# A recurrence with a MoE behind it: b's own load buffer, earlier load requests, and pair rows evicted into the tile that they were made from

## The chip, the cores and the metric

One core of one Trainium2 chip runs the whole kernel in one launch. The metric is device microseconds of that launch. The engines go by short names: PE (TensorE, matrix multiply; PEld is its weight load), DVE (VectorE), ACT (ScalarE), POOL (GpSimd) and SP (SyncE, which here only issues DMA transfers). Each engine takes its own list of instructions in order.

## The reference

Per batch and head (4 x 8 = 32 of them) a state of 40 x 40 is carried over 768 time steps; the outputs go through a feed-forward layer with a piecewise activation.

```
for t in range(S):
    y[:, :, t] = einsum('bhd,bhde->bhe', r_t, state)
    Sa = einsum('bhde,bhe->bhd', state, a_t)
    state = state * w_t[:, :, None, :] - einsum('bhd,bhe->bhde', Sa, b_t) + einsum('bhd,bhe->bhde', v_t, k_t)
x = y as (batch * time, 320)
h = x @ w_in                      # 320 -> 2048
g = h if h >= 1, 0 if h <= -1, else (h + 1)^2 / 4
out = g @ w_out                   # 2048 -> 320
```

## The kernel before, in words

The recurrence is done in chunks of 32 steps (24 chunks), so that inside a chunk it is matrix products, with a unit triangular system to invert. Four chunks (128 steps) make a segment; there are six segments, 0 to 5. Segments 0 and 1 are prepared by code of their own ahead of the main loop (`early_load`, `early_products`, `early_turn`, `early_ab`, `early_store`); segments 2 to 5 go through three background generators that run beside the main loop.

**Rows** (`prelude`, lines 217 to 262). For a segment, decayed and rescaled versions of k, w, a and b are worked out in four parts of eight steps each. Tiles of 128 x 8 x 40 are loaded by `load` (line 225, on SP) into buffers of one copy each: `ld_w`, `ld_a`, `ld_k`. b has no buffer; it is loaded into `ld_a`, after a's last use. Per part: two copies of r and v in DRAM (`copy_rv`, line 123, SP); the running product P of w on DVE (lines 239 and 240 carry over from the part before and need the new a and w, line 243 goes on); `at` on POOL (245); the load of b (247); reciprocal and its running product `rec` on DVE (249, 252); `kt` on POOL (255); `bt` on POOL (257); the store of all four from one tile, `arena`, to a DRAM scratch (258, on POOL's DMA queue); then the loads of the next part's w, a and k (261). Lines 239 and 240 of the next part write `arena` again and so also wait for that store.

**Pairs** (`ab_set`, lines 276 to 309). For a chunk, a and b rows are read back into `tiab` (`load_rows`, line 274, four transfers on SP), turned by four DVE transposes of 128 x 256 into `ea` (287, one buffer, tag "ea"), multiplied pair by pair on PE (298, 32 matmuls into one bank of PSUM), copied by ACT into a tile `ab` (303, one buffer) and stored by four transfers on SP to the DRAM scratch `abd` (306). As soon as the transposes are emitted, the next chunk's `tiab` load is queued.

**Inverse** (`invert`, lines 311 to 336). A segment's triangular systems are loaded (316), solved by 62 operations on POOL (326 and 332; DVE for segment 0) and stored (335).

**The main loop** (lines 847 to 892) runs, per chunk and half of the heads, `chain` (six stages of PE matmuls at lines 468, 479, 497, 526 and 536, with evictions by DVE at 486, 504 and 509 and by ACT at 473, 490, 530 and 538), `scores` (PE 438, DVE 447), `turn` (DVE transposes 423, 426 and 428) and the loads for the chunks to come (`load_ti`, `load_cg`: lines 274, 398, 401, 409). Every 64 steps `relayout` queues nine transfers X<-Y on SP (552, 558, 562) that make the MoE's input. The MoE's matmuls (607 into `ph`, 581 and 585 into `po`, with evictions at ACT 613 and 614, DVE 620, ACT 594 and POOL 595) are fed into PE's list between the chain's stages, a fixed number of columns a step.

The order is written by hand: the pool's own scheduling is off, and the order in which the Python code emits instructions is the order on each engine. The background generators `yield` a cost after each piece (`ROWS_W`, `AB_W`, `INV_W`, and literals), and `background` draws, in each third of a step, from whichever generator is furthest behind its share of a window of steps (`WINDOWS`). Rows of a segment run beside the pairs of the segment before for segments 3 to 5; the last pairs, of segment 5, run alone. The costs only place the emission; they are not times.

The weights of the MoE are loaded and split into two parts by another generator, `weights`, which lends its staging room from tiles that are idle at that time (`reclaim` takes them back).

Of the kernel before, what the change touches and what calls it, by code (L numbers as in the profile page):

```python
# [9 lines left out]
F32 = mybir.dt.float32  # L10
# [18 lines left out]
    ab=[(0, 0), (38, 53), (68, 89), (108, 129), (147, 169)],  # L29
# [20 lines left out]
def rwkv_moe_kernel(ctx: ExitStack, tc: tile.TileContext, r, k, v, w, a, b, w_in, w_out, ident_d, mask_d, out):  # L50
# [8 lines left out]
    const = ctx.enter_context(tc.tile_pool(name="const", bufs=1))  # L59
# [7 lines left out]

    ident = const.tile([128, D], F32, name="ident")
    mask = const.tile([128, 32], F32, name="mask")
    half_c = const.tile([128, 1], F32, name="half_c")  # L70
    nc.gpsimd.memset(half_c, 0.5)
    zero_c = const.tile([128, 1], F32, name="zero_c")
    nc.gpsimd.memset(zero_c, 0.0)

    x_tile = lambda i, t: const.tile([128, 6, 256], t, name=f"X{i}", tag=f"X{i}")
# [16 lines left out]
    work = ctx.enter_context(tc.tile_pool(name="work", bufs=1))  # L92
# [10 lines left out]
    def pad_rows(x, n):  # L103
        for q in (1, 3):
            zero(x[32 * q : 32 * q + 32, :, n : n + 32], 32 * q)
# [14 lines left out]
    def copy_rv(s, part, c):  # L120

        x, o = ((r, O_R), (v, O_V))[part]
        nc.sync.dma_start(
            scr4[s][c, :, :, o : o + D], x.rearrange("b h (n t) e -> (b h) n t e", t=L)[:, 4 * s + c]
        )

    def pad_scr(s):
        nc.sync.dma_start(scr[s][NH * 128 : NH * 128 + 1, 0:D], r[0, 0, 0:1, :])
# [88 lines left out]
    def prelude(s):  # L217

        reclaim(8)
        R = arena.rearrange("p (t x) -> p t x", x=160)  # L220
        kt, P, at, bt = (R[:, :, 40 * i : 40 * i + 40] for i in range(4))

        def load(n, part, tag):
            t = work.tile([128, 8, D], F32, tag=f"ld_{tag}", name=f"ld_{n}")
            nc.sync.dma_start(t, srcs[n][:, 4 * s : 4 * s + 4, 8 * part : 8 * part + 8, :])
            return t

        wl, al, kl = load("w", 0, "w"), load("a", 0, "a"), load("k", 0, "k")
        pad_scr(s)
        yield 10  # L230
        for part in range(4):
            ts_ = slice(8 * part, 8 * part + 8)
            for i in range(2):
                copy_rv(s, i, part)
            if part == 0:
                for x, y in ((P, wl), (at, al)):
                    nc.vector.tensor_scalar(out=x[:, 0], in0=y[:, 0], scalar1=-1.0, scalar2=None, op0=ALU.mult)
            else:
                nc.vector.tensor_mul(at[:, 0], al[:, 0], P[:, 7])
                nc.vector.tensor_mul(P[:, 0], wl[:, 0], P[:, 7])  # L240
            for t in range(1, 8):
                yield 0.4
                nc.vector.tensor_mul(P[:, t], P[:, t - 1], wl[:, t])
            yield ROWS_W[0]
            nc.gpsimd.tensor_mul(at[:, 1:], al[:, 1:], P[:, :7])
            yield ROWS_W[1]
            bl = load("b", part, "a")
            rec = work.tile([128, 8, D], F32, tag="ld_rec", name="rec")
            nc.vector.reciprocal(rec[:, 7], P[:, 7])
            yield 0.6  # L250
            for t in range(7, 0, -1):
                nc.vector.tensor_mul(rec[:, t - 1], rec[:, t], wl[:, t])
                yield 0.4
            yield ROWS_W[2]
            nc.gpsimd.tensor_mul(kt, kl, rec)
            yield ROWS_W[3]
            nc.gpsimd.tensor_mul(bt, bl, rec)
            nc.gpsimd.dma_start(scr[s][0 : NH * 128, 80:240].rearrange("(p t) x -> p t x", t=L)[:, ts_, :], R)
            yield ROWS_W[4]
            if part < 3:  # L260
                wl, al, kl = load("w", part + 1, "w"), load("a", part + 1, "a"), load("k", part + 1, "k")
            yield ROWS_W[5]

    def load_rows(dst, c, off, n, h0=0, nh=NH):

        sc = scr[c // 4]
        for f in range(2):
            for q in range(2):
                row = (h0 + f) * 128 + 32 * (c % 4)
                m = n - 32 * q  # L270
                src = bass.AP(
                    sc.tensor, sc.offset + row * RW + off + 32 * q, [[RW, 32], [256 * RW, nh // 2], [1, m]]
                )
                nc.sync.dma_start(dst[64 * f + 32 * q : 64 * f + 32 * q + 32, :, 0:m], src)  # L274

    def ab_set(s):

        if 9 in lending:
            reclaim(9)
            pad_rows(tiab, 48)  # L280
        load_rows(tiab, 4 * s, O_A, 80)
        yield AB_W[4]
        for c in range(4 * s, 4 * s + 4):
            ea = work.tile([128, 16, 2, 32], F32, tag="ea", name="ea")
            tv = tiab.rearrange("p h (j x) -> p h j x", x=40)[:, :, :, 0:32]
            for i in range(4):
                nc.vector.transpose(ea[:, 4 * i : 4 * i + 4], tv[:, 4 * i : 4 * i + 4])
                yield AB_W[0]
            if c < 4 * s + 3:
                load_rows(tiab, c + 1, O_A, 80)  # L290
            yield AB_W[1]
            ps = psum()
            for p in range(16):
                for f in range(2):
                    rows = slice(64 * f, 64 * f + D)
                    q = 2 * f + p % 2
                    sl = p // 2
                    nc.tensor.matmul(
                        ps[32 * q : 32 * q + 32, 32 * sl : 32 * sl + 32],
                        lhsT=ea[rows, p, 0, :], rhs=ea[rows, p, 1, :], start=True, stop=True,  # L300
                    )
            ab = work.tile([128, 8, 32], F32, tag="ab", name="ab")
            nc.scalar.copy(ab, ps[:, 0:256].rearrange("p (s x) -> p s x", x=32))
            yield AB_W[2]
            for q in range(4):
                nc.sync.dma_start(
                    abd[c // 4][q // 2, c % 4, q % 2 :: 2].rearrange("h t i -> t h i"), ab[32 * q : 32 * q + 32]
                )
            yield AB_W[3]
# [28 lines left out]
    def staged(key, needs, work_of):  # L338
# [12 lines left out]
    done, size, spent = dict(rows=1, ab=1), dict(rows=10 + 4 * (6.2 + sum(ROWS_W)), ab=AB_W[4] + 4 * (4 * AB_W[0] + sum(AB_W[1:4])), inv=INV_W + 67), {}  # L351
    back = {k: staged(*a) for k, a in dict(
        rows=("rows", None, prelude), ab=("ab", "rows", ab_set), inv=("inv", "ab", invert)).items()}

    def drain(key, s):
# [365 lines left out]
    def reclaim(kind):  # L721

        lending.discard(kind)
        while any(x[0] == kind for x in sts.values()):
            next(wgen)
# [10 lines left out]
    load = lambda q: loader[0](q)  # L736
# [189 lines left out]
```

## Time and profile before

| what | us |
|---|---|
| three timed runs | 978.39 median, 973.5 to 979.82 |
| the profiled execution, its own time | 976.18 |
| its span in the trace | 974.4 |
| PE busy in the span | 775.0 (80%) |
| DVE, ACT, POOL busy | 590.4, 478.6, 443.8 |
| mean granted TensorE clock | 0.85 of full |

Lines of the profile read as follows. In a timeline a row has start and length in us, engine, source line, operation, what it writes and reads (`out<-in`), the shapes, how many instructions are merged (x4), and in brackets how long the engine was idle before the first of them and what ended that idle time. A list of waits has who waited, what for, the total in us, how often, and the longest. "SPq" is SP issuing a transfer; the time beside it is that of issuing, not of the transfer.

### The profile page before, as it was taken

Reading aid. Unit: us, or ns where it says so; the run is one execution under the profiler, and the core shown is the slowest. Engines: PE = TensorE matmul, PEld = TensorE weight load, DVE = VectorE, ACT = ScalarE, POOL = GpSimd, SP = SyncE. Lnnn points to the kernel's source line nnn. Section 1 sums busy time; section 2 is a strip of 40 time slices with the busy share of each in tenths; the row PEclk is TensorE's granted clock in tenths of the full one; section 3 lists DMA queues with packets and bytes.
Section 4 is the critical chain, followed back from the end, with each engine's and each line's share of the span. In section 5 each row is a group of like instructions: output and inputs, shape, how many; then the busy total and the mean of one; then the engine's idle time right before and its main releaser. Section 6 shows DMA issues by size and latency. Waiting matters only on the chain.

```text
span 974.4 us, 35827 instructions
## 1 busy us (share of the span) xinstructions
PE 775.0 (80%) x14976; PEld 692.1 (71%) x14976; DVE 590.4 (61%) x1562; ACT 478.6 (49%) x1230; POOL 443.8 (46%) x673
## 2 busy tenths in 40 slices
PE   4523543447886988799879798989999999999995
PEld 3312532336776887688879687978898899999995
DVE  7782876574756583775654774776665556655321
ACT  5822444212543544454445454546565566656663
POOL 5200223686331599332588232697235962222332
PEclk9755555575997789797999796999999999999998
DMA  8799995565677755896735886856855545552010
GB/s 274 148 193 245 202 207 151 141 139 134 146 156 152 163 138 115 178 186 130 179 100 117 182 160 133 173 135 131 146 115 121 110 101 111 105 90 56 16 36 14
DMA packets 276866, 134.64 MB, mean 138 GB/s; under 512 B 194984, under 2 KB 266856, under 8 KB 276704
## 3 DMA queue, kind: packets, MB, share of 16 engines
q1 hardware_dynamic: 273504, 121.20, 57.9%
q0 software_dynamic: 3200, 11.14, 3.8%
q8 instruction: 118, 1.93, 0.9%
q14 instruction: 44, 0.36, 0.1%
HBM read 96.83 MB, written 33.82 MB: 134 GB/s over the span
## 4 chain that ended last, share of the span: by engine, by line
PE 34%; DMA 16%; POOL 16%; DVE 12%; issue 8%; SPq 8%; ACT 4%; POOLq 0%; ACTq 0%; DVEq 0%
PE ph L607 11%; PE po L581 6%; POOL lw L326 5%; POOL lw L332 4%; DMA ti<-scr 4%; PE po L585 3%; PE p L497 3%; POOL gl L595 3%; SPq L274 3%; PE p L468 3%; PE p L526 2%; DMA ld_a<-in_a_dram 2%; PE p L438 2%; PE p L479 2%; PE p L536 1%
## 5 line engine op out<-in xcount | busy, mean ns | idle before, releaser
L607 PE MATMUL ph<-X,w 120*128 120x256 f32 x1536 | 260.9, 307 | 51.6 <-DVE qt L620 44.3
L595 POOL TENSOR_TENSOR gl<-qt,gh 128x256 fp32r<-128x256 f32 x192 | 140.9, 734 | 280.0 <-ACT gh L594 264.6
L607 PEld LDWEIGHTS ph<-X,w 120*128 120x128 f32 x1536 | 219.8, 203 | 68.1 <-DVE qt L620 51.3
L620 DVE SCALAR_TENSOR_TENSOR qt<-qt,ph 128x256 f32<-128x256 f32 x192 | 79.9, 416 | 150.3 <-ACT qt L614 148.3
L581 PE MATMUL po<-wide,gh 128*128 128x320 f32 x768 | 163.7, 329 | 0.3 <-ACT gh L594 0.3
L594 ACT CAST gh<-qt 128x256 fp32r<-128x256 f32 x192 | 78.0, 406 | 167.6 <-DVE qt L620 166.7
L581 PEld LDWEIGHTS po<-wide,gh 128*128 128x128 f32 x768 | 124.6, 202 | 3.7 <-ACT gh L594 0.5
L613 ACT ACTIVATE qt<-ph,half_c 128x256 f32<-128x256 f32 x192 | 91.1, 474 | 53.4 <-POOL gl L595 39.7
L585 PE MATMUL po<-wide,gl 128*128 128x320 f32 x384 | 99.6, 338 | 17.6 <-POOL gl L595 17.6
L497 PE MATMUL p<-cg 128*64 128x72 f32 (+1 forms) x1536 | 74.8, 262 | 44.2 <-DVE cg L486 39.7
L497 PEld LDWEIGHTS p<-cg 128*64 128x64 f32 x1536 | 66.8, 166 | 54.3 <-ACT cg L490 45.0
L326 POOL TENSOR_TENSOR lw<-lw 128x31 f32<-128x31 f32 (+15 forms) x155 | 94.4, 609 | 18.0 <-DMA lw<-abd 9.3
L490 ACT ACTIVATE cg<-p 32x160 f32<-32x160 f32 x192 | 56.8, 296 | 87.9 <-DVE cg L486 61.0
L447 DVE TENSOR_TENSOR cg<-p,mask 32x256 f32<-32x256 f32 x192 | 80.6, 420 | 25.8 <-PE p L438 23.2
L332 POOL TENSOR_TENSOR lw<-lw 128x31 f32<-128x31 f32 (+15 forms) x155 | 84.1, 543 | 8.8
L504 DVE SCALAR_TENSOR_TENSOR cg<-p,pr 40x160 f32<-40x160 f32 x184 | 59.1, 321 | 41.1 <-PE p L497 39.2
L614 ACT ACTIVATE qt<-qt 128x256 f32<-128x256 f32 x192 | 80.2, 418 | 6.1
L585 PEld LDWEIGHTS po<-wide,gl 128*128 128x128 f32 x384 | 65.6, 197 | 23.9 <-POOL gl L595 21.5
L468 PE MATMUL p<-cg 128*64 128x72 f32 x1536 | 66.4, 243 | 16.7 <-DMA cg<-ttd 15.0
L486 DVE SCALAR_TENSOR_TENSOR cg<-p,mask 32x128 f32<-32x128 f32 x192 | 55.2, 288 | 36.2 <-PE p L479 30.7
L468 PEld LDWEIGHTS p<-cg 128*64 128x64 f32 x1536 | 58.7, 149 | 23.6 <-issue 19.0
L526 PE MATMUL p<-ident,cg 40*64 40x40 f32 x1472 | 57.1, 238 | 1.9 <-issue 1.9
(104 smaller groups left out, 1027.9 us busy)
## 6 DMA issues: line engine op xcount, KB each, us to landing
ti<-scr SPq DMA_DIRECT2D x96, 200.0 KB
ti<-scr SPq DMA_DIRECT2D x96, 168.0 KB
scr<-arena POOLq DMA_DIRECT2D x16, 640.0 KB, 5.4
cg<-scr SPq DMA_DIRECT2D x96, 80.0 KB
X<-Y SPq DMA_DIRECT2D x36, 160.0 KB
scr<-wide SPq DMA_DIRECT2D x8, 640.0 KB
tiab<-scr SPq DMA_DIRECT2D x32, 160.0 KB
scr<-in_r_dram SPq DMA_DIRECT2D x24, 160.0 KB
```

Of the source, the lines that this page charges most:

```text
L326: eng.tensor_mul(t3, W3[:, 0:n, j : j + 1].broadcast_to([128, n, m]), L3[:, j + 1 :, j].unsqueeze(1).broadcast_to([128, n, m]),)
L332: eng.tensor_sub(W3[:, 0:n, j + 1 :], W3[:, 0:n, j + 1 :], t3)
L447: nc.vector.tensor_tensor(out=cg[q, f::2, C_X : C_X + 64][:, 4 * i : 4 * i + 4].rearrange("p h (j x) -> p h j x", x=32), in0=ps[quarter(f, ...
L468: nc.tensor.matmul(psv[h // 8][64 * (1 - f) : 64 * (1 - f) + 64, h // 2 % 4, 0:72], lhsT=cg[:, h, C_T : C_T + 64], rhs=cg[:, h, C_R : C_R ...
L497: nc.tensor.matmul(psv[h // 8][64 * f : 64 * f + 64, h // 2 % 4, 0:n3], lhsT=cgw[:, h * CW + C_G : h * CW + C_G + 64], rhs=cg[:, h, C_R : ...
L581: nc.tensor.matmul(pos[i], lhsT=gh[:, ts_], rhs=w2[f // 8][:, j, f % 8, :], start=f == 0 and j == 0, stop=False)
L585: nc.tensor.matmul(pos[i], lhsT=gl[:, ts_], rhs=w2[f // 8][:, 0, f % 8, :], start=False, stop=f == NF - 1)
L595: nc.gpsimd.tensor_sub(gl, gt, gh.bitcast(F32))
L607: nc.tensor.matmul(ph, lhsT=w1[:, wi, fs], rhs=Xs[g][:, xi, :], start=i == 0, stop=i == 7)
L613: nc.scalar.activation(gt, ph, AF.Relu, bias=half_c, scale=0.5)
L614: nc.scalar.activation(gt, gt, AF.Square)
L620: nc.vector.scalar_tensor_tensor(out=gt, in0=gt, scalar=1.0, in1=ph, op0=ALU.min, op1=ALU.max)
```

## The change

The load buffers become four: b's loads go into `ld_b`. A part's b is no longer asked for in the middle of the part but with the loads of the part before (or, for part 0, at the start). The next part's loads are asked for one by one: a after the last `rec` product is emitted, w after `kt`, k and b after `bt` and the store. The planner's costs and the number of yields stay as they were, so everything else is emitted in the same order.

In the pairs, the tile `ab` goes; the PSUM bank is copied into the first half of `ea`, over rows that the matmuls have read, and the four stores read from there. The two constants 0.5 and 0 share one tile of two columns.

```
-    half_c = const.tile([128, 1], F32, name="half_c")
+    consts = const.tile([128, 2], F32, name="consts")
+    half_c, zero_c = consts[:, 0:1], consts[:, 1:2]
...
-        wl, al, kl = load("w", 0, "w"), load("a", 0, "a"), load("k", 0, "k")
+        wl, al, kl, bl = (load(n, 0, n) for n in "wakb")
...
             nc.gpsimd.tensor_mul(at[:, 1:], al[:, 1:], P[:, :7])
             yield ROWS_W[1]
-            bl = load("b", part, "a")
             rec = work.tile([128, 8, D], F32, tag="ld_rec", name="rec")
...
+            more = part < 3
+            if more:
+                al = load("a", part + 1, "a")
             yield ROWS_W[2]
             nc.gpsimd.tensor_mul(kt, kl, rec)
+            if more:
+                wl = load("w", part + 1, "w")
             yield ROWS_W[3]
             nc.gpsimd.tensor_mul(bt, bl, rec)
             nc.gpsimd.dma_start(scr[s][0 : NH * 128, 80:240].rearrange("(p t) x -> p t x", t=L)[:, ts_, :], R)
             yield ROWS_W[4]
-            if part < 3:
-                wl, al, kl = load("w", part + 1, "w"), load("a", part + 1, "a"), load("k", part + 1, "k")
+            if more:
+                kl, bl = load("k", part + 1, "k"), load("b", part + 1, "b")
             yield ROWS_W[5]
...
-            ab = work.tile([128, 8, 32], F32, tag="ab", name="ab")
+            ab = ea.rearrange("p a j x -> p (a j) x")[:, 0:8]
             nc.scalar.copy(ab, ps[:, 0:256].rearrange("p (s x) -> p s x", x=32))
```

More of the change, by code (lines that the diff above doesn't have):

```diff
@@ L69, in rwkv_moe_kernel @@
     mask = const.tile([128, 32], F32, name="mask")
-    half_c = const.tile([128, 1], F32, name="half_c")
+    consts = const.tile([128, 2], F32, name="consts")
+    half_c, zero_c = consts[:, 0:1], consts[:, 1:2]
     nc.gpsimd.memset(half_c, 0.5)
-    zero_c = const.tile([128, 1], F32, name="zero_c")
     nc.gpsimd.memset(zero_c, 0.0)
```

## The prediction

> **What bounds the kernel now.** I read the page first, then a table of stretches, then the list of waits, then the timeline around each wait that the change removes or adds.
>
> ```profile
> span 974.4 us, 35827 instructions
> ...
> PEclk9755555575997789797999796999999999999998
> ...
> scr<-arena POOLq DMA_DIRECT2D x16, 640.0 KB, 5.4
> ```
> ```profile
> 708.00:728.00 20.00, 20.00 (x438) 18.15 (x440) 12.11 (x34) 13.39 (x36) 5.62 (x8) 1.00 0.57 118
> 728.00:912.00 184.00, 181.48 (x3672) 164.54 (x3668) 105.92 (x282) 110.36 (x292) 83.02 (x130) 0.99 0.44 93
> ```
>
> From 728 us on, PE is busy 181.48 us of 184 at a granted clock of 0.99, and nothing that the change touches runs any more after the last rows and pairs are done. (Columns: the stretch and its length, busy time of PE, PEld, DVE, ACT and POOL, granted clock, DMA share, GB/s.) Before that PE has holes, and the clock row of the page dips with them. Every engine here runs a fixed list in order, so a hole in PE moves the end by its length, and a wait on another engine costs only what reaches PE. That is the rule by which I price everything below.
>
> ```profile
> DVE arena L239 <- DMA ld_a<-in_a_dram: 24.9, 5, 12.1
> ...
> POOL arena L257 <- DMA ld_b<-in_b_dram: 18.4, 7, 6.9
> DVE ea L287 <- DMA tiab<-scr: 18.4, 6, 6.0
> ...
> ACT ab L303 <- DMA abd<-ab: 5.6, 2, 4.1
> ```
>
> (Columns: us in total, times, the longest.) The first two lines are what the change goes for: DVE waits 24.9 us in five places for the next part's a, POOL 18.4 us in seven for b. The fourth goes too: the eviction waited twice for the old tile's stores. The third says that DVE already sits at the pair transposes until a load lands: the very place where the change puts one wait more.
>
> **What the change removes.** The 16 parts of the rows (segments 2 to 5, four each) issue the same 64 loads and as many vector instructions; only their places differ. With b in its own buffer, a load of a is queued after the reciprocals, w after the k product, k and b after the b product, so no part waits for its own b, and a and w stand several planner units earlier in SP's queue. Issuing costs the same; the two constants in one tile cost nothing, for nothing in the loops writes them. At the start of a segment's rows one load more (b) is queued behind w, a and k, and is not the one that is waited for first.
>
> I go through the waits that end.
>
> ```profile
> 188.35 0.96 POOL L258 DMA_DIRECT2D scr<-arena  x1 [0.30 <-POOL arena L257]
> ...
> 196.77 0.20 DVE L239 TENSOR_TENSOR arena<-ld_a,arena 128x40 f32<-128x40 f32 x1 [5.30 <-DMA ld_a<-in_a_dram]
> ...
> 207.69 2.08 PE L607 MATMUL ph<-X,w 120*128 120x256 f32 x8 [9.84 <-DVE qt L620]
> ...
> 236.01 0.93 POOL L258 DMA_DIRECT2D scr<-arena  x1 [0.30 <-POOL arena L257]
> ...
> 242.26 0.20 DVE L239 TENSOR_TENSOR arena<-ld_a,arena 128x40 f32<-128x40 f32 x1 [12.06 <-DMA ld_a<-in_a_dram]
> ...
> 244.96 1.09 PE L607 MATMUL ph<-X,w 120*128 120x256 f32 x7 [1.37 <-DVE qt L620]
> ```
>
> L239 is also the first to overwrite the arena that the previous part's store is reading, so **the store is late next**. At 196.77 that store was issued at 188.35 and takes 5.4 us (the page's median): 193.75, so 3.0 of the 5.30 us are won, and PE's hole of 9.84 shrinks by them. At 242.26 the store ends at 236.01 + 5.4 = 241.4: of 12.06 us only 0.9 are won. Two other such waits, 1.89 us at 419.80 and 5.13 us at 449.80, stand beside a PE without a hole:
>
> ```profile
> 419.80 0.20 DVE L239 TENSOR_TENSOR arena<-ld_a,arena 128x40 f32<-128x40 f32 x1 [1.89 <-DMA ld_a<-in_a_dram]
> ...
> 449.08 2.08 PE L607 MATMUL ph<-X,w 120*128 120x256 f32 x8
> ...
> 449.80 0.20 DVE L239 TENSOR_TENSOR arena<-ld_a,arena 128x40 f32<-128x40 f32 x1 [5.13 <-DMA ld_a<-in_a_dram]
> ...
> 466.43 1.22 PE L607 MATMUL ph<-X,w 120*128 120x256 f32 x8
> ...
> 468.36 0.86 POOL L257 TENSOR_TENSOR arena<-ld_b,rec 128x320 f32<-128x320 f32 x1 [6.89 <-DMA ld_b<-in_b_dram]
> ...
> 471.26 0.90 PE L585 MATMUL po<-wide,gl 128*128 128x320 f32 x2 [2.29 <-POOL gl L595]
> ...
> 471.96 1.91 PE L607 MATMUL ph<-X,w 120*128 120x256 f32 x8
> ```
>
> They count as 0 here (1.9 + 5.1 if the cover, matmuls already queued, is gone). Of POOL's waits for b the one of 6.89 us reaches PE: gl is late behind it and PE waits 2.29 us. It also costs clock: eight matmuls of L607 take 1.91 us after the hole and 1.22 before it, 0.7 us more. So 3.0 us are won there. The waits of 6.15 us at 315.53 and 2.35 at 582.66 (below) have no such hole behind them. **Won: 3.0 + 0.9 + 3.0 = 6.9 us**; at least 0 (SP's order may hold the moved loads as late), at most the 22.4 us of the first rival.
>
> **What the change adds.** The eviction now writes the first half of ea, and four stores on SP's queue read it. With one buffer of ea, the next chunk's first transpose (L287) must wait until those stores have landed; before, only the next eviction had to. Behind L287 on DVE stand the next L620 (the MoE's evictions, which PE's L607 and L581 need) and the chain's L447, L423 and L486. How long a store takes to land is seen in the two places where the eviction waited for it: it ran at 447.60 and 315.23, that is 1.5 and 4.85 us after the fourth issue had ended (443.03 + 3.03, 306.46 + 3.92). I take 1.5 and keep 4.85 for the range. There are 12 such boundaries, three a segment. At five the stores come late: at 293.09, 438.41, 582.31 and 713.87 a relayout's nine X<-Y issues (L552 to L562) stand ahead of them on SP, and at 308.98 the stores of one chunk later are still behind:
>
> ```profile
> 293.09 1.42 DVE L287 STREAM_TRANSPOSE ea<-tiab 128x256 f32<-128x256 f32 x4 [6.00 <-DMA tiab<-scr]
> ...
> 297.46 0.80 PE L607 MATMUL ph<-X,w 120*128 120x256 f32 x2 [4.37 <-DVE qt L620]
> ...
> 297.82 3.44 SPq L306 DMA_DIRECT2D abd<-ab  x4
> ...
> 306.46 3.92 SPq L306 DMA_DIRECT2D abd<-ab  x4
> ...
> 308.98 1.38 DVE L287 STREAM_TRANSPOSE ea<-tiab 128x256 f32<-128x256 f32 x4
> ...
> 315.23 0.37 ACT L303 COPY ab<-p 128x256 f32<-128x256 f32 x1 [4.12 <-DMA abd<-ab]
> ...
> 315.53 0.87 POOL L257 TENSOR_TENSOR arena<-ld_b,rec 128x320 f32<-128x320 f32 x1 [6.15 <-DMA ld_b<-in_b_dram]
> ...
> 438.41 1.38 DVE L287 STREAM_TRANSPOSE ea<-tiab 128x256 f32<-128x256 f32 x4
> ...
> 443.03 3.03 SPq L306 DMA_DIRECT2D abd<-ab  x4
> ...
> 445.86 1.08 PE L298 MATMUL p<-ea 40*32 40x32 f32 x64
> ...
> 447.60 0.37 ACT L303 COPY ab<-p 128x256 f32<-128x256 f32 x1 [1.45 <-DMA abd<-ab]
> ...
> 582.31 1.42 DVE L287 STREAM_TRANSPOSE ea<-tiab 128x256 f32<-128x256 f32 x4
> ...
> 582.66 0.88 POOL L257 TENSOR_TENSOR arena<-ld_b,rec 128x320 f32<-128x320 f32 x1 [2.35 <-DMA ld_b<-in_b_dram]
> ...
> 586.60 2.91 SPq L306 DMA_DIRECT2D abd<-ab  x4
> ...
> 592.00 1.08 PE L298 MATMUL p<-ea 40*32 40x32 f32 x64
> ...
> 713.87 1.38 DVE L287 STREAM_TRANSPOSE ea<-tiab 128x256 f32<-128x256 f32 x4
> ...
> 715.54 1.90 SPq L306 DMA_DIRECT2D abd<-ab  x4
> ...
> 718.40 0.76 PE L298 MATMUL p<-ea 40*32 40x32 f32 x64
> ```
>
> At 293.09 the stores land at 297.82 + 3.44 + 1.5 = 302.8, 9.7 us late, and PE was already idle for the L620 behind these transposes (4.37 us): **9.7 us**, all of it a longer hole. At 308.98 they landed about when the eviction ran, 315.23: 6.25 us late; SP, which doesn't wait for DVE there, catches up while the stall before it lasts, so I take half, **3.1** (0 to 6.25). At 438.41 PE doesn't need the transposes before its L298 at 445.86; they would end at 447.6 + 1.4 = 449.0: **3.1**. PE's clock is down there anyway (2.08 us for eight, above). At 582.31 they would end at 586.60 + 2.91 + 1.5 + 1.4 = 592.4, L298 was at 592.00: **0.4**. At 713.87 they would end between 720.3 and 723.7, L298 was at 718.40: 1.9 to 5.3, the middle 3.6, and 0.7 for the clock, which is full there: **4.3**. The other boundaries have stores that land about when the transposes start, and PE's L298 well behind. **Lost: 20.6 us**. With 4.85 in place of 1.5 it would be 13.1, 6.25 (whole), 6.5, 3.8 and 6.0: 35.6; at the least the 9.7 us of the first rival.
>
> The sum: 20.6 - 6.9 = 13.7 us slower. The profiled execution took 976.18 us, so 989.9; it lies 2.2 us under the median of the runs shown (978.39), within their spread, and I say **990 us**.
>
> The Trainium skill (TensorE: Matmul & The Clock Gate, "Why this matters for your kernels") asks for no PE idle gaps over about 3 us, since one window of idleness (about 3.4 us by its Part 1, "The HAM clock gate") halves the clock; here a hole of 2.29 us was enough, so the trace is stricter. By the page's window, half of 3.4 us, 1.7 us, would be an estimate of the loss per new hole of 3 us (the second and the last, 3.4 in place of 0.7), and nothing for the one of 2.29, which makes the sum 17.1.
>
> **The rivals.**
> 1. Faster, by SP's queue running ahead. If the earlier loads leave SP 6 us ahead at 297.82, the stores cost 4 us there, nothing at 308.98 and 582.31, 3.1 at 438.41 and 1.9 + 0.7 at 713.87: 9.7. If also each removed wait counts whole (3.0, 0.9, 1.9, 5.1, 3.0, and b's 6.15 and 2.35): 22.4. That is 976.2 - 12.7 = 963.5 us. For it: the size of the two waits. Against: the load before the store is moved within the same queue, and PE shows no hole behind most of these waits. It decides if the stores at 297.82 go out before about 292.
> 2. A wash: 6.9 won, and 10.0 lost (5 at 293.09, nothing at 308.98 and 582.31, 3.1 and 1.9 at the other two), if SP gains half of what rival 1 wants: 979 us. For it: while DVE stalls, SP goes on, and the list behind it finds its loads done. Against: the stall lasts until just those stores land, so SP is no further ahead at its end than its own issues.
> 3. Slow landings: 35.6 lost, 6.9 won: 1005 us. For it: one of the two landings that show is the slow one. Against: the other was a third of it, behind the same nine issues that stand ahead of most.
> 4. The change doesn't do what it says: SP takes its list in order, so a load queued earlier behind a waiting issue comes as late, and nothing is won: 976.2 + 20.6 = 997 us.
>
> **How the numbers follow.** A difference of 1%, 9.8 us, is about what a measurement of this kernel can tell from no change. Forecast 0.38, with a range of its own of 983 to 998, of which 0.12 lies within 1%; rival 1 0.20; rival 2 0.20; rival 3 0.12; rival 4 0.10. Faster by over 1%: 0.20; within 1%: 0.12 + 0.20 = 0.32; slower: 0.26 + 0.12 + 0.10 = 0.48. The range of 8 in 10 runs from just above rival 1 to rival 3: 965 to 1006.
>
> **What would show it.** Right: no waits of L257 for ld_b, those of L239 for ld_a replaced by shorter ones for scr<-arena; waits of L287 for the stores, some 30 to 45 us in all on DVE, longest near 300; and a PE hole near 300 of over 10 us. Wrong: L287 waits less than 15 us in all for the stores (SP ran ahead: rival 1 or 2), or L239 still waits for ld_a (rival 4). If the waits come as said and the time doesn't follow, the step that failed is that PE's holes are what counts.

## The result and the profile after

| | us | over before |
|---|---|---|
| before, beside the first runs of after | 977.92 median | |
| after, 4 runs (978.52 to 991.24) | 988.87 median | 1.0115, 95% interval 1.0068 to 1.0161 |
| after, timed again beside other kernels, 6 runs | 986.88 median | 1.0104, 1.0050 to 1.0159 |
| the profiled execution of after, and its span | 989.62, 987.8 | |

The change makes the kernel about 1.1% slower; the prediction was 990 us. Here and below medians count every run, and ratios leave out the few runs of a second, slower state, so the two need not agree to a tenth of a per cent. From the page of after, the clock by slices (24.7 us each), and then its list of waits:

```profile
PEclk9755555676977798896989798977989999999998
```
```profile
DVE ea L291 <- DMA abd<-ea: 53.3, 11, 12.7
...
PE p L302 <- DVE ea L291: 8.4, 4, 3.5
...
DVE ea L291 <- DMA tiab<-scr: 6.4, 1, 6.4
```

In the 11th to the 30th slice (some 245 to 740 us) the clock is under 9 tenths in 12, against 7 before; behind them both are full but for the last slice. In the list (from line 247 on, a line of before stands four lines lower in after: the transposes are L291, the pairs' matmuls L302, their stores L310, the MoE's evictions L624, its first matmuls L611) POOL's 18.4 us for b are gone (L257 now waits 5.2 us in four places for `rec`). Of DVE's 24.9 us for a one wait is left, 11.2 us. In their place the transposes wait 53.3 us for the stores, in 11 of the 12 boundaries; some of that was the wait for tiab before (18.4 us, now 6.4). The row of PE has grown: PE waits for those transposes 8.4 us in four places, against 1.8 us in two before.

The timeline of after, at the places that the prediction named:

```profile
193.56 0.39 DVE L239 TENSOR_TENSOR arena<-ld_a,arena 128x40 f32<-128x40 f32 x1 [2.28 <-DMA scr<-arena]
...
194.09 3.14 DVE L243 TENSOR_TENSOR arena<-arena,ld_w 128x40 f32<-128x40 f32 x7
...
206.19 2.08 PE L611 MATMUL ph<-X,w 120*128 120x256 f32 x8 [8.37 <-DVE qt L624]
...
232.37 0.35 SPq L339 DMA_DIRECT2D ttd<-lw  x1
...
235.87 0.99 SPq L225 DMA_DIRECT2D ld_a<-in_a_dram  x1
...
239.66 0.20 DVE L239 TENSOR_TENSOR arena<-ld_a,arena 128x40 f32<-128x40 f32 x1 [11.15 <-DMA ld_a<-in_a_dram]
...
296.34 2.05 SPq L310 DMA_DIRECT2D abd<-ea  x4
...
299.73 1.42 DVE L291 STREAM_TRANSPOSE ea<-tiab 128x256 f32<-128x256 f32 x4 [12.66 <-DMA abd<-ea]
...
304.11 0.79 PE L611 MATMUL ph<-X,w 120*128 120x256 f32 x2 [8.50 <-DVE qt L624]
...
307.84 4.08 SPq L310 DMA_DIRECT2D abd<-ea  x4
...
313.19 0.64 PE L611 MATMUL ph<-X,w 120*128 120x256 f32 x4
...
316.76 1.42 DVE L291 STREAM_TRANSPOSE ea<-tiab 128x256 f32<-128x256 f32 x4 [3.48 <-DMA abd<-ea]
...
317.35 1.14 PE L302 MATMUL p<-ea 40*32 40x32 f32 x54 [3.52 <-DVE ea L291]
...
456.46 1.43 DVE L291 STREAM_TRANSPOSE ea<-tiab 128x256 f32<-128x256 f32 x4 [9.86 <-DMA abd<-ea]
...
457.05 1.33 PE L302 MATMUL p<-ea 40*32 40x32 f32 x64 [0.83 <-DVE ea L291]
...
598.25 1.33 PE L302 MATMUL p<-ea 40*32 40x32 f32 x64 [1.80 <-DVE ea L291]
...
730.23 1.42 DVE L291 STREAM_TRANSPOSE ea<-tiab 128x256 f32<-128x256 f32 x4 [6.26 <-DMA abd<-ea]
...
730.82 1.33 PE L302 MATMUL p<-ea 40*32 40x32 f32 x64 [2.26 <-DVE ea L291]
```

Read a wait of L291 together with the PE row behind it. The wait of 12.66 us has a PE hole of 8.50 behind it (4.37 before), the one of 9.86 only 0.83, the one of 6.26 has 2.26. The length of a wait on DVE says little about what PE loses.

**Two profiles of the kernel before.** A stage can't be compared here from one pair of traces, as a second profile of the unchanged kernel shows.

> The kernel before, profiled once more. If the clock's dips follow from the order of the work alone, every stage has the clock and length that it had (24.7 us at 0.65 between the chain halves near 581 and 606, 15.1 us at 1.00 between 653 and 669, a hole of 2.29 near 471). If they are partly chance, some stages with equal waits differ by 3 to 8 us between the two profiles of the same kernel.

The stages lie between the same halves of the chain in each profile, so that they hold the same matmuls, within one or two that a trace can lack. A row has the stretch and its length, the busy time of PE, PEld, DVE, ACT and POOL with their counts, the granted clock, the DMA share and GB/s. The first profile of before (976.18 us):

```profile
261.31:329.99 68.68, 57.45 (x1098) 50.45 (x1097) 37.71 (x120) 26.69 (x72) 18.74 (x25) 0.80 0.77 163
...
459.66:477.19 17.53, 15.24 (x282) 13.80 (x281) 8.85 (x27) 7.58 (x20) 6.00 (x11) 0.90 0.68 187
...
653.40:668.46 15.06, 14.34 (x281) 12.55 (x281) 6.00 (x15) 8.46 (x23) 14.20 (x22) 1.00 0.73 158
713.16:727.76 14.60, 14.60 (x346) 13.19 (x345) 8.86 (x24) 10.07 (x27) 3.92 (x6) 1.00 0.58 108
727.76:756.33 28.57, 27.74 (x561) 25.01 (x560) 17.29 (x48) 15.99 (x43) 15.88 (x30) 1.00 0.48 107
```

The second (980.76 us):

```profile
260.45:325.39 64.94, 54.56 (x1098) 47.98 (x1097) 37.77 (x120) 26.57 (x72) 18.71 (x25) 0.82 0.77 164
...
462.06:476.20 14.14, 13.82 (x281) 12.52 (x280) 8.01 (x22) 7.43 (x20) 4.79 (x6) 1.00 0.75 205
...
727.87:763.98 36.11, 33.63 (x562) 30.34 (x561) 17.28 (x48) 16.09 (x43) 19.41 (x35) 0.81 0.39 86
```

The last row: the same matmuls took 28.57 us at a clock of 1.00 and 36.11 at 0.81. The first row differs by 3.7, the second by 3.4. So the clock's dips are partly chance, worth 3 to 8 us in a stage. What a change is worth must come from the times, or from stages in which many profiles agree; one trace shows where waits and holes went. The Trainium skill (TensorE: Matmul & The Clock Gate, "What's actually happening") says that the window over which the clock judges idleness runs free of the kernel's start; these two profiles fit that, without showing that it is the reason.

### The profile page after: what moved, and what is told of

It is laid out like the page before. It is cut to its first block, busy times and chain, and to the rows that moved or that the text cites. A ratio compares the mean times of both kernels' runs of the same rounds, so it can differ in the third digit from the quotient of the medians.

```text
span 987.8 us, 35849 instructions
## 1 busy us (share of the span) xinstructions
PE 781.2 (79%) x14976; PEld 697.5 (71%) x14976; DVE 592.9 (60%) x1562; ACT 476.8 (48%) x1230; POOL 442.8 (45%) x673
## 3 DMA queue, kind: packets, MB, share of 16 engines
q8 instruction: 118, 1.93, 0.9%
## 4 chain that ended last, share of the span: by engine, by line
PE 31%; POOL 17%; DMA 14%; DVE 14%; SPq 10%; issue 8%; ACT 3%; DVEq 0%; POOLq 0%; ACTq 0%
PE ph L611 10%; POOL lw L330 6%; PE po L585 5%; POOL lw L336 5%; PE po L589 3%; POOL gl L599 3%; PE p L501 2%; DMA cg<-scr 2%; PE p L530 2%; SPq L278 2%; DMA ti<-scr 2%; SPq L562 2%; PE p L472 2%; PE p L483 2%; PE p L540 2%
## 5 line engine op out<-in xcount | busy, mean ns | idle before, releaser
L611 PE MATMUL ph<-X,w 120*128 120x256 f32 x1536 | 262.8, 309 | 52.9 <-DVE qt L624 49.3
L611 PEld LDWEIGHTS ph<-X,w 120*128 120x128 f32 x1536 | 221.4, 205 | 69.7 <-DVE qt L624 53.8
L624 DVE SCALAR_TENSOR_TENSOR qt<-qt,ph 128x256 f32<-128x256 f32 x192 | 79.7, 415 | 137.6 <-ACT qt L618 132.9
L617 ACT ACTIVATE qt<-ph,consts 128x256 f32<-128x256 f32 x192 | 90.9, 474 | 43.6 <-POOL gl L599 32.8
L501 PE MATMUL p<-cg 128*64 128x72 f32 (+1 forms) x1536 | 69.6, 250 | 41.8 <-DVE cg L490 41.8
L501 PEld LDWEIGHTS p<-cg 128*64 128x64 f32 x1536 | 62.0, 156 | 51.7 <-ACT cg L494 42.6
L472 PEld LDWEIGHTS p<-cg 128*64 128x64 f32 x1536 | 57.6, 146 | 23.3 <-issue 18.7
L530 PE MATMUL p<-ident,cg 40*64 40x40 f32 x1472 | 60.0, 244 | 3.4 <-issue 3.4
```

What stands on the lines that cost most here:

```text
L472: nc.tensor.matmul(psv[h // 8][64 * (1 - f) : 64 * (1 - f) + 64, h // 2 % 4, 0:72], lhsT=cg[:, h, C_T : C_T + 64], rhs=cg[:, h, C_R : C_R ...
L501: nc.tensor.matmul(psv[h // 8][64 * f : 64 * f + 64, h // 2 % 4, 0:n3], lhsT=cgw[:, h * CW + C_G : h * CW + C_G + 64], rhs=cg[:, h, C_R : ...
L530: nc.tensor.matmul(pst[64 * f : 64 * f + 64, p, :], lhsT=cn[er[f], h, C_S : C_S + 64], rhs=ident[er[f]], start=True, stop=True)
L611: nc.tensor.matmul(ph, lhsT=w1[:, wi, fs], rhs=Xs[g][:, xi, :], start=i == 0, stop=i == 7)
L617: nc.scalar.activation(gt, ph, AF.Relu, bias=half_c, scale=0.5)
```

## The experiments

All ratios are over the kernel before, run on the same chip beside each kernel; a tenth of a per cent is 1 us.

**Each part alone.** The eviction alone:

```
-            ab = work.tile([128, 8, 32], F32, tag="ab", name="ab")
+            ab = ea.rearrange("p a j x -> p (a j) x")[:, 0:8]
```

> The kernel before with the eviction alone changed (into the first half of ea, own tile gone); the loads stay as they were. Theory: the stall of the next transposes (L287) behind the stores is the whole loss, and the loads win something on their own; so this one is slower than the whole change: 18 to 22 us over before, 996 to 1000 us, with L287 waiting 45 to 60 us in all for the stores and a PE hole of over 8 us near 300. Rival A, the loads win nothing: as the whole change, 988 to 990 us. Rival B, the difference of the whole change comes from when the clock dips and not from the stall: 976 to 982 us with the waits of L287 there all the same.

Measured: 986.92 us, ratio 1.0119 (1.0082 to 1.0157). The transposes wait 44.3 us for stores, PE's hole near 300 is 9.23 us. The eviction costs 11.6 us, less than the 18 to 22 expected and more than rival B allows. That is what the whole change costs (10.2 and 11.2 us), so rival A is nearest: beside the eviction the gain of the loads doesn't show.

The loads alone. The eviction goes to columns of `lw` that lie idle between two inverses, so it needs no tile of its own:

```
-            ab = ea.rearrange("p a j x -> p (a j) x")[:, 0:8]
+            ab = lw[:, 2048:2304].rearrange("p (s x) -> p s x", x=32)
```

> The whole change, but the eviction goes to 1 KB a partition of its own, the last 256 columns of lw, which the inverse uses as scratch at other times; so the loads' part alone. Theory: 6 to 9 us under before, 969 to 972 us, no waits of L291 for stores, PE's hole near 207 about 8.4 in place of 9.84 us, the one at 471 gone. Rival A, SP takes its list in order, so the loads win nothing that lasts: 976 to 980 us. Rival B, SP ahead and every removed wait counts whole: 22 us won, 956 us.

Measured: 972.20 us, ratio 0.9962 (0.9933 to 0.9991): 3.7 us won. In its list of waits, and in its timeline at the places of the first gain and the first loss:

```profile
ACT lw L307 <- DMA abd<-lw: 6.9, 3, 3.3
```
```profile
206.47 2.07 PE L611 MATMUL ph<-X,w 120*128 120x256 f32 x8 [8.19 <-DVE qt L624]
...
293.20 1.42 DVE L291 STREAM_TRANSPOSE ea<-tiab 128x256 f32<-128x256 f32 x4 [6.66 <-DMA tiab<-scr]
```

Without the stores in the way the transposes near 293 run when they did before (293.09). The evictions wait for the stores of the chunk before, as they did in `ab`. So the change has a good half and a bad half, and the prediction had the signs of both. The good half is small: its interval ends just under 1.

**Which boundaries.** The same kernel with the eviction back in `ea` in some chunks (c is the round; c = 9 stands ahead of boundary A at 293, 10 of B at 309, 14, 18 and 22 of C, D and E), or in `lw` only in those five:

```
             ab = lw[:, 2048:2304].rearrange("p (s x) -> p s x", x=32)
+            if c == 9:
+                ab = ea.rearrange("p a j x -> p (a j) x")[:, 0:8]
```

> Loads as in the whole change; the eviction goes to the 256 columns of lw in all chunks but one, the second of segment 2 (c = 9), which goes into the first half of ea. So only the transposes near 293 wait for stores. Theory, a boundary costs the hole that it makes in PE: that boundary alone cost 8.5 us (eviction change alone) and 10.9 us (whole change) between two chain halves, so 8.5 to 11 us over the loads' part alone, 980 to 983 us, with one wait of L291 of 12 to 13 us. Rival, the loss is spread over all the waits by their length: 12.7 of 53.3 us of some 15, 3.6 us, 975 to 976 us. Rival, what is lost there is given back by a better clock later: 971 to 974 us.

> The whole change, with the eviction into the 256 columns of lw in the five chunks whose stores were predicted to come late (c = 9, 10, 14, 18, 22) and into ea in the other eleven. Theory: these five carry the whole loss, so the time is that of the loads' part alone, 969 to 974 us, and what is left of L291's waits (15 us or less) stands beside busy matmuls. Rival, all waits count by their length: 14.7 of 53.3 us are left, 4 us, 975 to 978 us.

> Loads as in the whole change; the eviction goes into ea in chunks c = 9 and 10 alone (the waits near 293 and 309), elsewhere into the 256 columns of lw. Chunk 9 alone measured 0.9976 of before, 0.14% over the loads' part alone. Theory now, the loss does not add boundary by boundary: a wait costs little by itself and much when a second follows on it before the clock is back, so A and B together cost most of the loss: 8 us over the loads' part, 979 to 983 us. Rival, the prediction's sizes (9.7 + 3.1 = 12.8 us): 984 to 987 us. Rival, A and B cost what A alone did and the loss sits at the other three: 973 to 976 us.

> Loads as in the whole change; the eviction goes into ea in chunks c = 14, 18 and 22 alone (the waits near 438, 582 and 714), elsewhere into lw. Theory now, most of the loss is at A and B, and these three cost the rest, 3 to 6 us over the loads' part: 975 to 979 us. The prediction's sizes: 3.1 + 0.4 + 4.3 = 7.8 us, 979 to 982 us. Rival, the loss sits here: 11 us or more, 983 to 987 us.

| eviction into ea at | us | ratio (interval) | over the loads alone |
|---|---|---|---|
| none (the loads alone) | 972.20 | 0.9962 (0.9933 to 0.9991) | |
| A | 973.83 | 0.9976 (0.9951 to 1.0002) | 1.4 us |
| A, B | 981.53 | 1.0043 (1.0008 to 1.0078) | 7.9 us |
| C, D, E | 975.16 | 0.9990 (0.9961 to 1.0020) | 2.7 us |
| all but A to E | 973.94 | 0.9965 (0.9933 to 0.9997) | 0.3 us |

The waits of the last of these:

```profile
DVE ea L291 <- DMA abd<-ea: 15.8, 7, 4.6
```

The last column is the difference of the ratios times 977 us; each is good to about 4 us. The last row fits that the five late boundaries carry the loss: with the other seven alone the kernel is as fast as the loads alone, though their transposes wait those 15.8 us. (That expectation's rival, 4 us for them, lies at the edge of what these times can tell.) A and B with C, D and E make 10.6 us, close to the 11.6 of the eviction alone.

How the loss divides between A and B the times don't settle. They give A 1.4 us, good to 3.8 (980 to 983 us had been expected for it), and B with A ahead of it 6.5 us more, good to about 4.2; B alone was not run. The stages say otherwise. These are the two up to A's end, in the loads alone and then with A in `ea`:

```profile
259.63:279.24 19.61, 17.61 (x346) 15.72 (x345) 13.39 (x46) 8.46 (x23) 6.96 (x9) 0.83 0.87 178
279.24:304.59 25.35, 18.20 (x409) 15.67 (x409) 10.99 (x34) 9.48 (x27) 4.42 (x6) 0.87 0.71 158
```
```profile
259.53:274.88 15.35, 14.87 (x346) 13.20 (x345) 10.66 (x37) 8.45 (x23) 6.05 (x8) 1.00 0.86 174
274.88:310.88 36.00, 22.61 (x410) 19.71 (x409) 16.36 (x52) 10.23 (x29) 6.02 (x8) 0.67 0.67 142
```

Each pair sums to 44.96 and 51.35 us. The same sums and stages in every profile so far and in those below, all but the kernel with stores from ACT:

| stretch | eviction not in ea there | in ea there |
|---|---|---|
| the two stages up to A's end | 43.9 to 45.3 us, six profiles | 50.2 to 51.9 us, seven |
| the stage of B | 19.8 to 24.8, seven | 23.1 to 28.0, six |
| the stage of E and the one behind it | 42.1 to 52.3, seven | 42.8 to 51.1, six |

A costs 6.5 us in the mean, and no profile of one kind lies near one of the other. B costs some 3 us in the mean, with the two kinds overlapping, and E nothing that shows once the stage behind it is counted. By the stages A and B make 9.6 us, by the times 7.9. What gives the kernel with A alone its good time all the same isn't known. That B finds the clock still low from A can be ruled out as the reason for its price: at 313.19, in the timeline of after above, four L611 take 0.64 us, about half of what eight take at full clock (1.22 us, at 466.43 in before).

**Why the stores are late.** Two ways to have them sooner. From ACT, which has just made the data:

```
-                nc.sync.dma_start(
+                nc.scalar.dma_start(
                     abd[c // 4][q // 2, c % 4, q % 2 :: 2].rearrange("h t i -> t h i"), ab[32 * q : 32 * q + 32]
```

> The whole change, with the four stores of each chunk's pairs issued by ACT, right behind the eviction or the work that ACT has next in its list, in place of SP. Theory: what made the stores late is the SP queue (relayout issues ahead of them), so L291 waits under 10 us in all for the stores, the hole near 304 falls under 4 us, and the time goes to 968 to 976 us, under before. Rival: issuing four stores takes ACT as long as it takes SP (1.9 to 3.9 us), 16 times, and the copies and activations behind them come late, so that PE's holes move there: 984 to 995 us.

Measured: 1018.07 us, ratio 1.0434 (1.0405 to 1.0464), worse than every other version. Its list of waits, and ACT and its queue in its timeline:

```profile
DVE ea L291 <- DMA tiab<-scr: 51.9, 11, 7.8
```
```profile
285.25 1.93 ACTq L310 DMA_DIRECT2D abd<-ea  x4
...
287.22 0.40 ACT L598 CAST gh<-qt 128x256 fp32r<-128x256 f32 x1 [2.00 <-issue]
```

The theory held at A and B, whose stretch takes 64.60 us here (68.68 and 64.94 in the two profiles of before), and fell elsewhere, in two ways. The transposes don't wait for the stores any more, but 51.9 us for the load of tiab, which SP issues (18.4 in the kernel before): by its list of waits SP now sits still for the stores that ACT issues, 69.3 us ahead of L413, L405 and L278 (none in after), so that what it issues comes late; PE waits 21.6 us for X, against 3.6 in after. And while ACT issues, for 1.93 us, the copy that POOL and PE need stands behind it: the rival's mechanism, at over its price. All 64 issues take ACT some 31 us, at 1.93 for four. How the loss of 42 us divides between the two was not tried apart. The Trainium skill (DMA: Bandwidth & Descriptors, "Issuing engines are not separate DMA queues") says that starting transfers from several engines saves only the issuing time, usually small beside the transfer. Here that time, 1.93 us for four, was not small beside the 1.3 us that the stores at A took to land after their issue on SP, and on ACT it is not free.

Or queued sooner on SP, by the planner's costs:

```
-AB_W = (1, 6, 3, 8, 15)
+AB_W = (1, 6, 0, 11, 15)
```

> The whole change with the planner's costs of the pairs (1, 6, 0, 11, 15) in place of (1, 6, 3, 8, 15): a chunk's stores are queued right behind its eviction. On SP they then stand ahead of the relayout (X<-Y) at the boundaries near 438, 582 and 714, and not at 293, where SP is busy without a gap from 270 to 298. Theory: SP's place is the price at those three and at 309, so 1.5 + 3 + 6 of loss go and the 10.9 us at 293 stay: 979 to 983 us. Rival, the stores now wait at SP's head for the eviction, and the relayout behind them comes late: 990 to 1000 us.

Measured: 986.59 us, ratio 1.0124 (1.0087 to 1.0162), no better than after. Its list of waits, and its timeline at boundary E:

```profile
DVE ea L291 <- DMA abd<-ea: 28.7, 7, 12.4
```
```profile
720.58 2.83 SPq L310 DMA_DIRECT2D abd<-ea  x4
...
723.50 2.37 SPq L556 DMA_DIRECT2D X<-Y  x3
...
725.68 1.38 DVE L291 STREAM_TRANSPOSE ea<-tiab 128x256 f32<-128x256 f32 x4
...
728.71 0.71 PE L611 MATMUL ph<-X,w 120*128 120x256 f32 x4 [1.31 <-DMA X<-Y]
```

The transposes' waits fall from 53.3 to 28.7 us, and at E there is none left; but the relayout now stands behind the stores, and PE's L611 waits for X instead. With that hole of 1.31 us the stage is as long as it was in after (20.32, below):

```profile
724.98:745.88 20.90, 19.21 (x345) 16.87 (x344) 9.23 (x25) 10.37 (x28) 4.32 (x6) 0.76 0.44 97
```

The rival's mechanism was right, its price was not. The wait only changed its name. Such a hole isn't the work of the stores alone, though: with A alone, whose stores at E are in `lw` and behind the relayout, PE waits there for X too, and the stage takes 18.92 us at a clock of 0.82:

```profile
718.53 0.38 PE L613 MATMUL ph<-X,w 120*128 120x256 f32 x1 [1.10 <-DMA X<-Y]
```

**Less behind the wait.**

```
-            for i in range(4):
+            for i in (1, 2, 3, 0):
                 nc.vector.transpose(ea[:, 4 * i : 4 * i + 4], tv[:, 4 * i : 4 * i + 4])
```

> The whole change, with the four transposes of a chunk in the order 1, 2, 3, 0: only transpose 0 writes what the stores read, so three of four (about 0.35 us each) and the DVE work between them can run before the wait. Theory: the wait ends when it did, and 1 us less stands behind it at each of the boundaries where PE waits (five or six): 3 to 6 us under the whole change, 983 to 986 us. Rival, DVE work between the transposes was waiting too and the whole stall is hidden: 975 to 979 us. Rival, the stores land as late and transpose 0 is followed at once by PE's matmuls, nothing won: 988 to 990 us.

Measured: 990.37 us, ratio 1.0156 (1.0118 to 1.0195): the last rival, nothing won. The wait for the stores stays at 52.0 us, and what PE waits for those transposes goes from 8.4 to 11.5 (6.7 in the second profile of after).

**A better version.** Four pieces of `lw`, so that the evictions don't wait for stores either:

```
+            at = (2048, 0, 256, 512)[c % 4]
+            ab = lw[:, at : at + 256].rearrange("p (s x) -> p s x", x=32)
```

> Loads as in the whole change, and each of the four chunks of a segment evicts to 256 columns of its own in lw (the scratch, and three pieces of the part into which the inverse loads only after all four are stored). So neither the transposes nor the next eviction wait for stores. Theory: ACT's three waits for stores in the loads' part alone (6.9 us in all) go, but only one of them had a PE hole behind it (1.37 us at 429), so 970 to 972 us. Rival, the waits of ACT count whole: 965 us. Rival, the evictions into the inverse's input wait for the inverse to end: 974 to 980 us.

Measured: 972.06 us, ratio 0.9976 (0.9945 to 1.0008), not to be told from the single piece: ACT's 6.9 us for stores were hidden. The loads with one piece of `lw` (0.9962) is the version to keep: the simpler of the two, and ahead of both kernels.

**After once more.**

> The kernel after, timed again beside the others of this call and profiled once more. Theory: 1.0115 of before, as before (988 us), with the stage between the halves near 280 and 305 long again (over 33 us, clock under 0.7) and the one of 714 to 728 long (20 us). If the 7 us lost near 661 were chance, that stage is 14 to 15 us this time.

Measured: 986.88 us, ratio 1.0104. The stage near 661 and that of boundary E in the first profile of after:

```profile
657.32:679.35 22.03, 19.87 (x281) 17.86 (x280) 8.76 (x24) 10.11 (x27) 20.35 (x33) 0.69 0.62 115
723.20:743.52 20.32, 18.06 (x345) 15.99 (x345) 9.24 (x25) 10.05 (x28) 4.29 (x6) 0.83 0.44 82
```

These two in its second profile, and E's wait in its timeline:

```profile
666.70:680.41 13.71, 13.71 (x281) 12.47 (x281) 7.08 (x19) 9.44 (x25) 12.77 (x21) 1.00 0.70 123
725.87:741.13 15.26, 14.99 (x345) 13.32 (x345) 8.81 (x24) 9.70 (x27) 3.86 (x6) 1.00 0.53 98
```
```profile
729.98 1.42 DVE L291 STREAM_TRANSPOSE ea<-tiab 128x256 f32<-128x256 f32 x4 [3.34 <-DMA abd<-ea]
```

The 7 us near 661 were chance (13.71 us this time). The stretch of A and B is long again (76.43 us and now 78.29, against 64.94 and 68.68 of before). E is 20.32 us with a hole of 2.26 and 15.26 where the wait of 3.34 us was covered by matmuls. The kernel with C, D and E alone gives a third size:

```profile
719.69 1.33 PE L302 MATMUL p<-ea 40*32 40x32 f32 x64 [3.29 <-DVE ea L291]
```
```profile
711.10:734.46 23.36, 20.07 (x346) 18.07 (x345) 10.07 (x28) 10.15 (x28) 5.17 (x7) 0.71 0.41 77
```

Against 14.60 us without a hole, the stage with one of 2.26 is 5.7 us longer and that with one of 3.29 is 8.8: more than twice the hole, the rest being the clock (1.00, 0.83, 0.71). Whether that lasts is another matter: the stage behind takes 27.49 us in all three of these profiles, and 28.57 and 36.11 in the two of before.

## Why the prediction was right, point by point

The net (13.7 us) came out at 10 to 11 us because both terms were sized too large, by nearly the same factor: the loss was 11.6 us by the eviction alone (predicted 20.6), the gain 3.7 by the loads alone (predicted 6.9). The runs of the parts make 7.9 us, the whole change 10.2 and 11.2; their intervals overlap. That the net is off by only some 3 us where the loss is off by 9 is in part luck: the gain, sized too large as well, takes some of it back, and the whole change measured a little more than its parts.

**The gain.** At 196.77 the step held: the arena's store is late next. It was predicted to end at 193.75, and L239 ran at 193.56, 3.2 us sooner. But PE's hole went from 9.84 to 8.37 (8.19 with the loads alone), half of it. The step that failed is "PE's hole of 9.84 shrinks by them": the seven products behind it (L243) took longer. From the timeline of before, and from that of after, on POOL:

```profile
197.12 1.61 DVE L243 TENSOR_TENSOR arena<-arena,ld_w 128x40 f32<-128x40 f32 x7
...
198.57 0.79 POOL L245 TENSOR_TENSOR arena<-ld_a,arena 128x280 f32<-128x280 f32 x1 [2.10 <-DVE arena L243]
```
```profile
195.49 0.75 POOL L330 TENSOR_TENSOR lw<-lw 128x240 f32<-128x240 f32 x1
```

They took 1.61 us beside a POOL that sat idle for 2.10 us until they were done, and 3.14 in after, where POOL's inverse still runs beside them. The 1.53 us and 0.19 more on L239 are the whole of what is missing. The second profiles of before and after show the same, 1.60 us and 3.13. The Trainium skill (SBUF — State Buffer, "Who interferes with whom") says that a DVE instruction with two SBUF inputs contends with a GpSimd instruction that reads SBUF; the rows agree.

At 242.26 the wait shrank by 0.9 us, as said, but not for the reason given, and PE has little of it: L239 still waits for a (11.15 us), not for the arena's store, and PE's hole behind it goes from 1.37 to 1.31 us. The rows at 232.37 and 235.87 show that the load stands on SP behind the store of the inverse, which waits for POOL. That is rival 4, at this one place. The 3.0 us at 471.26 were read wrongly. In the second profile of before POOL waits for b there again, and PE hardly notices:

```profile
468.78 0.88 POOL L257 TENSOR_TENSOR arena<-ld_b,rec 128x320 f32<-128x320 f32 x1 [5.80 <-DMA ld_b<-in_b_dram]
...
471.69 0.56 PE L585 MATMUL po<-wide,gl 128*128 128x320 f32 x2 [0.32 <-POOL gl L595]
```

5.80 us of wait, 0.32 of hole, and a stage of 14.14 us like that of every later kernel. The 2.29 us were that one execution's. So 1.5 of the 3.7 us have a place, the hole near 207; the rest lies within what the times can tell.

**The loss.** The places A and B were right, A was sized too large, and of C, D and E the runs show little.
- A, 9.7 predicted. L291 ran on the stores at 299.73, not at 302.8: SP issued them 1.5 us sooner and in 2.05 us in place of 3.44. The transposes were 6.6 us late, PE's hole grew by 4.1 (4.37 to 8.50). The stages give A 6.5 us, the times of the kernel with A alone 1.4, at the most some 5.
- B, 3.1 predicted as half of 6.25. PE's hole at L302 is 3.52 (1.40 before), DVE's wait 3.48. The stages give it some 3 us, the times 6.5 with A ahead of it. Its stores needed 4.08 us to issue and 4.8 more to land (307.84 + 4.08 to 316.76): the slow landing of rival 3, as in before (4.85), and at this one place.
- C, D and E, 3.1 + 0.4 + 4.3 = 7.8 predicted, 2.7 measured, good to about 4. At C 9.86 us of wait left a hole of 0.83, at D there is one of 1.80. E's hole (2.26) is in the predicted 1.9 to 5.3 and makes its stage 5.7 us longer when it comes, but it doesn't always come (3.34 us of wait and none in the second profile), and with the stage behind it no loss shows.

**What would show it.** L257's waits for b are gone, as said; L291 waited 53.3 us, more than the 30 to 45 said (41.9 in the second profile); the hole near 300 was 8.50 (7.91), not over 10. The rule that PE's holes count and other waits don't was not contradicted: 15.8 us of DVE waits at the other seven boundaries cost 0.3 us and 6.9 us of ACT waits nothing, each good to about 4 us. What it lacked is that a hole's price is its length and the clock behind it, that the second part differs from run to run, and that what one stage loses need not last. Rival 1's waits that count whole are refuted by the loads alone (3.7 us, not 22.4). The estimate by the window of the Trainium skill (TensorE: Matmul & The Clock Gate), 1.7 us of clock for a new hole of 3 us, is too low for the hole of 3.29 at E: 8.8 less 3.29 are 5.5 us in that stage.

## What to carry to other kernels

Reusing a tile that a store still reads makes the next writer wait for the store (53.3 us here), and the store waits for everything ahead of it on its queue; look for a piece of memory that is idle in that phase (here the inverse's scratch) before giving up a buffer. Price a wait by the hole that it leaves in the engine that bounds the stage, then add the clock, and look whether the stage behind gives some of it back. Profile the unchanged kernel twice before reading a difference of a few us in a stage; when several variants share a stage, compare it over all their profiles. A queue is a list: moving one entry ahead puts the next one behind, and moving it to another engine's queue can leave the first queue waiting for it.

## What the runs showed of the hardware

- The stage of boundary E ran at a clock of 0.82 with a hole of 1.10 us in PE, 0.76 with one of 1.31, 0.83 with one of 2.26, 0.71 with one of 3.29, and 1.00 with a DVE wait of 3.34 us that left PE busy.
- Seven DVE products of 128x40 take 1.61 us beside an idle POOL and 3.14 beside its inverse.
- Issuing the four stores of a chunk takes 1.9 to 4.1 us on SP and 1.9 on ACT; the transposes that wait for them run 1.3 us after the last issue at A and 4.8 at B, in the same execution.
